# Mamba-2 scan and expert merge on one core: outputs of two pairs of chunks in one TensorE visit, the state term in 32x32 tiles

## The chip, the cores and the metric

One core of a Trainium2 chip. The metric is the device time of the kernel in microseconds (us), the median of several executions. TensorE is called PE here, VectorE DVE, ScalarE ACT, GpSimd POOL, and SyncE, which issues nearly all transfers, SP.

## The reference

Two parts run one after the other, all in float32. First a state-space scan (4 sequences, 8 heads, 768 positions, 32 channels and 16 states per head), written in chunks:

```python
L = np.exp(cum[:, :, :, None] - cum[:, :, None, :]) * causal   # decay from j to i
CB = np.einsum('bhin,bhjn->bhij', Cc, Bc)
y_intra = np.einsum('bhij,bhjd->bhid', CB * L, xc)
y_inter = np.einsum('bhin,bhnd->bhid', Cc, state) * np.exp(cum)[:, :, :, None]
y[:, :, sl] = y_intra + y_inter
state = decay_full[:, :, None, None] * state + np.sum(Bx, axis=2)
```

Then four experts over the 3072 rows of 256 values that the scan gives:

```python
p = domain_probs / (domain_probs.sum(-1, keepdims=True) + 1e-09)
for e in range(4):
    h = np.maximum(x @ w1[e], 0.0)          # 256 -> 1024
    out += p[:, e:e + 1] * (h @ w2[e])      # 1024 -> 256
```

## The kernel before

The scan runs in 24 chunks of 128 positions, numbered so that chunks 4i to 4i+3 are the i-th chunk of the four sequences. A chunk holds all 8 heads. Its work:

- `fetch` loads the chunk's x, B and C (tile xb), its decays spread over all partitions (ab) and, from chunk 4 on, its decays by head (ah).
- `decays` makes the decay matrix LT with two scans on DVE (L455), the decayed B in MT on POOL (`fade`, L461), the masked C in ctm on ACT (`mask`, L436), and from chunk 4 on the running decay dec (DVE, L735) and the decayed C, cts (POOL, L738).
- `scores` multiplies B and C on PE in four tiles of 32x128 (`score`, L443). It fills four PSUM banks with two chunks; then DVE multiplies each quarter of each chunk by LT into MT (`masked`, L600), eight instructions of 128x256 for a pair.
- `outputs` multiplies on PE, for two chunks: the state term, two 64x64 tiles a chunk (L774), and the part inside the chunk with the chunk's own new state, eight matmuls of 128x32 a chunk (`inner`, L468). ACT copies the outputs to yT (L790) and the new state to A (`keep_state`, L475 to L478).
- `carry` turns A on DVE (L806), adds the decayed old state (L808) and spreads the result S over a block-diagonal M by a product with qmask (L811), which the 64x64 tiles need, as two heads share a tile.

In odd chunks (`turned_round`) the halves of B, C and the decays are loaded the other way round, so that the odd chunk's state term uses the two 64x64 tiles that the even chunk leaves free.

The experts work on blocks of 4, 4, 4, 6 and 6 chunks (B, B, B, H, H) by a scheme that saves block products at the price of sums: sums of weights (L919), of tokens (L938) and of results (L857, L1136). Every product is L830, two matmuls of 128x128 by 128x256. ACT copies partial sums out of PSUM (snapshots, L839 and L1085) and into it (seeds, L844). DVE applies the gates (L865). Weights that are sums are stored once (L924) and loaded again (L916).

A block's work comes in units (a pair or a triple of weight blocks). `PAIRS_AT` says in which unit of a block the next block's pairs of chunks are made; within a unit the scores are put at position SC = 1 of the list of products and the outputs at OUT = 14:

```python
for x, make in ((SC, scores), (OUT, outputs)):
    mark = len(line)
    make(cs)
    at[x] = line[mark:]
```

The order of PE's work (`line`) is written out by this code. The order on every other engine is made by a planner (`Plan`) while the program is built: it walks through time with an assumed cost for each piece of work, assumed distances between engines (HOP), an assumed landing of transfers (RATE, LANDING) and an allowance after a landing before another engine's instruction on it is placed (MARGIN). It also hands out buffers: NV tiles v for values, NW tiles w for weights, eight PSUM banks. On the chip each engine takes its instructions strictly in the planned order.

Of the kernel before, what the change touches and what calls it, by code (L numbers as in the profile page):

```python
# [12 lines left out]
P = 128  # L13
# [5 lines left out]
HOP = 0.2  # L19
LANDING = 2.2  # L20
KEEP = 5
NV, NW = 33, 32
SC, OUT = 1, 14
# [4 lines left out]
RATE, MARGIN = 310.0, 4.0  # L28
AFTER = 1
HELD = ("x", "w"), (5, 8), (0, 7)  # L30
LAST = (0, 1), (0, 2), (1, 1), (1, 2), (0, 0), (1, 0)
LATE = (13, 2), (6, 9), (11, 4), (10, 12), (3,), (1, 14), ("x", "w"), (5, 8), (0, 7)
PAIRS_AT = {(3, 2): {0: 0, 1: 1}, (4, 2): {0: 0, 2: 1}, (4, 3): {0: 0, 1: 1, 2: 2},
            (6, 3): {0: 0, 2: 1, 3: 2}}
# [7 lines left out]
class Value:  # L42
    def __init__(self, kind, seeded=False, fills=True):
        self.kind, self.seeded, self.fills = kind, seeded, fills
        self.home, self.writers, self.readers, self.left, self.end = None, [], [], 0, 0.0

# [14 lines left out]
class Plan:  # L61
# [12 lines left out]
    def add(self, on, fn, reads=(), writes=(), part=(), lag=0.0, due=None, reuse=None, two=False,  # L74
            port=True, after=None, kb=0):
        w = Work(on, fn, lag)
        w.two, w.port, w.after, w.kb = two, port, after, kb
# [14 lines left out]
        for v in dict.fromkeys([*reads, *writes, *part]):  # L92
            w.touched.append(v)
            v.left += 1
# [8 lines left out]
    def times(self, line, at):  # L103
# [5 lines left out]
        for w in reversed(self.all):  # L109
            us = min(w.on.values()) + w.lag  # L110
            last = [f.latest - HOP for f in w.feeds]
            if "PE" in w.on:
                last.append(w.nominal + us)
            elif not last:
                last.append(t if w.due is None else w.due().nominal)
            w.latest = min(last) - us
# [46 lines left out]
    def run(self, line, at, begin):  # L163
# [17 lines left out]
        self.stall, self.port, self.bus = [], 0.0, 0.0  # L181
        while todo:
            e = min(t, key=lambda e: t[e])
            now = t[e]
            best, soon = None, None
            late = self.late = max(0.0, t["PE"] - line[head].nominal) if head < len(line) else 0.0
            for w in waiting[e]:
                if w.start is not None or e == "PE" and w.place != head:
                    continue
                ready = max([w.ready, w.after.nominal + late if w.after else 0.0] + [  # L190
                    n.end + (MARGIN if n.kb and e != "SP" else 0.0 if n.by == e and not n.kb else HOP)
# [19 lines left out]
                elif soon is None or when < soon:  # L211
                    soon = when
# [20 lines left out]
            if w.kb:  # L233
                self.bus = max(self.bus, t[e] + 1.6) + w.kb / RATE
                w.end = self.bus + .6
# [73 lines left out]
def kernel(  # L309
# [36 lines left out]
    def turned_round(c):  # L346
        return c >= NSEQ and c % 2 == 1
# [17 lines left out]
    def some(n, shape, name, pool=const):  # L365
# [9 lines left out]
        "LT": some(2, [P, NH, P], "LT"),  # L375
        "MT": some(2, [P, NH, P + N], "MT"),
        "ctm": some(2, [HN, NT, P], "ctm"),
        "cts": some(2, [HN, NT, P], "cts"),
        "dec": some(4, [HN, P], "dec"),
        "A": some(4, [P, NT, N], "A"),  # L380
        "S": some(6, [HN, D], "S"),
        "M": some(6, [HN, NQ, D], "M"),
# [8 lines left out]
    def load_tokens(c, xb):  # L391
        src = xbc[real(c)]
        if turned_round(c):
            nc.sync.dma_start(out=xb[:, :OBT], in_=src[:, :OBT])
            nc.sync.dma_start(out=xb[:HALF, OBT:], in_=src[HALF:, OBT:])
            nc.sync.dma_start(out=xb[HALF:, OBT:], in_=src[:HALF, OBT:])
        else:
            nc.sync.dma_start(out=xb, in_=src)
# [5 lines left out]
    def load_heads(c, ah):  # L404
        src = ac_d[real(c)].unsqueeze(1).to_broadcast([NH, N, P])
        if turned_round(c):
            nc.sync.dma_start(out=ah[:HALF], in_=src[NH // 2:])
            nc.sync.dma_start(out=ah[HALF:], in_=src[:NH // 2])
        else:
            nc.sync.dma_start(out=ah, in_=src)  # L410
# [38 lines left out]
    def quarter(c, r):  # L449
        q = r ^ 2 * turned_round(c)  # L450
        return slice(NT * q, NT * q + NT)

# [7 lines left out]
    def fade(c, MT, xb, LT):  # L460
        nc.gpsimd.tensor_mul(  # L461
            MT[:, :, P:], xb[:, OB:OB + HN].rearrange("p (h n) -> p h n", h=NH),
            LT[:, :, P - 1:P].to_broadcast([P, NH, N]))

    def inner(c, t, y, xb, MT, w, start):
        for q in range(NQ):
# [3 lines left out]
                rhs=MT[:, NT * q + t, 0:w], start=start, stop=True,  # L470
                tile_position=(0, 32 * q), skip_group_check=True)

    def keep_state(c, A, y):
        if c % 2:
            nc.scalar.copy(out=A[:HALF], in_=y[HALF:])  # L475
            nc.scalar.copy(out=A[HALF:], in_=y[:HALF])
        else:
            nc.scalar.copy(out=A, in_=y)  # L478
# [45 lines left out]
    qmask = const.tile([P, NQ, D], FP32)  # L524
    nc.vector.memset(qmask, 0.0)
    for q in range(NQ):
        nc.vector.memset(qmask[32 * q:32 * q + 32, q], 1.0)
# [61 lines left out]
    LT, MT, ctm = homes["LT"], homes["MT"], homes["ctm"]  # L589
# [74 lines left out]
    B512, B256 = {"DVE": .73, "POOL": 1.5}, {"DVE": .42, "POOL": .78}  # L664
# [7 lines left out]
    def dma(fn, n=1, kb=256, **kw):  # L672
        return plan.add({"SP": .38 * n}, fn, lag=LANDING + kb / 190, kb=kb, **kw)
# [15 lines left out]
    yT, gates, S, M = {}, {}, {}, {}  # L689
# [5 lines left out]
    st[3]["ab"] = plan.taken("ab", 0, now + 2)  # L695
    for c in range(2):
# [3 lines left out]
    def fetch(c):  # L700
        s = st[c]
        if "xb" not in s:
            s["xb"] = value("xb")
            dma(lambda e: load_tokens(c, s["xb"].t), 3 if turned_round(c) else 1, 320,
                part=[s["xb"]])
        if c >= NSEQ:
            s["ah"] = value("ah")
            dma(lambda e: load_heads(c, s["ah"].t), 2 if turned_round(c) else 1, 64,
# [5 lines left out]
    def decays(c):  # L714
        s = st[c]
        s["LT"] = value("LT")
        s["MT"] = value("MT")
        for part in range(2):
            if c < SPREAD:
                dve(1.25, lambda e, part=part: scan_quarters(  # L720
                    c, s["LT"].t, [b.t for b in s["a"]], part), reads=s["a"][2 * part:2 * part + 2],
                    part=[s["LT"]])
            else:
                half = NH * P // 2
                dve(1.25, lambda e, lo=half * part: scan(
                    s["LT"].t, s["ab"].t[:, lo:lo + half], lo), two=True, reads=[s["ab"]], part=[s["LT"]])
        if c < NCH - NSEQ:
            plan.add({"POOL": .43}, lambda e: fade(c, s["MT"].t, s["xb"].t, s["LT"].t),
# [671 lines left out]
```

## Time and profile before

| | |
|---|---|
| median of 3 runs | 631.25 us (630.66 to 634.42) |
| the profiled execution | 630.59 us, its span 628.8 us |
| PE busy | 622.6 us (99%) |
| DVE busy | 526.0 us (84%) |
| ACT busy | 261.9 us (42%) |
| POOL busy | 254.3 us (40%) |
| moved by DMA | 125.87 MB, mean 200 GB/s |

The span runs from the first to the last instruction. A group of the profile is named by its line in the kernel, its engine and operation, what it writes and reads, and its shape; the numbers are the busy time, the mean duration in ns, and the idle time of the engine just before it. In the chain of waits the last instruction is followed back to what released it. In the timeline each row has a start, a length, and a count of merged instructions; two records of PE belong to one float32 matmul.

### The profile page before, as it was taken

The page shows a single profiled execution, that of the slowest core. Times are in us where ns is not written, and L with a number is a line of the kernel's source. Part 1 is how long each engine was busy: PE and PEld are TensorE (multiplying, and loading weights), DVE is VectorE, ACT ScalarE, POOL GpSimd, SP SyncE. Part 2 cuts the span into 40 slices and gives each one's busy share as a digit, 9 for nine tenths or more (in the row PEclk, how much of TensorE's full clock was granted, in tenths as well). Part 3 has the DMA queues.
Part 4 walks back from the last instruction along what each step waited for, and adds up shares of the span by engine and source line. Part 5 has one row for each costly group of instructions (what it writes and reads, how often), then busy time and mean ns, then how long its engine had stood idle before and what let it go on. Part 6 is the DMA issues. An engine that isn't in the chain of part 4 may idle for free.

```text
span 628.8 us, 10190 instructions
## 1 busy us (share of the span) xinstructions
PE 622.6 (99%) x3363; PEld 529.3 (84%) x3363; DVE 526.0 (84%) x869; ACT 261.9 (42%) x538; POOL 254.3 (40%) x267
## 2 busy tenths in 40 slices
PE   9999999999999999999999999999999999999997
PEld 5787888888888888878888888888888888888886
DVE  7988899899997699988778988978787977768684
ACT  4222642434434353344433336355444235455441
POOL 4153552625534764543666421414045521233130
PEclk9999999999999999999999999999999999999999
DMA  7999795484898965699997827546123333951001
GB/s 206 307 304 346 231 302 197 123 282 126 287 336 298 315 189 164 173 322 334 349 365 244 280 63 250 176 118 199 57 80 94 101 73 80 361 176 47 1 1 51
DMA packets 110932, 125.87 MB, mean 200 GB/s; under 512 B 28692, under 2 KB 76832, under 8 KB 110880
## 3 DMA queue, kind: packets, MB, share of 16 engines
q1 hardware_dynamic: 110500, 124.97, 62.3%
q8 instruction: 27, 0.44, 0.3%
q10 hardware_dynamic: 380, 0.25, 0.1%
q14 instruction: 25, 0.20, 0.1%
HBM read 100.30 MB, written 24.89 MB: 199 GB/s over the span
## 4 chain that ended last, share of the span: by engine, by line
PE 93%; DMA 3%; DVE 2%; ACT 1%; issue 0%; SPq 0%; POOL 0%; ACTq 0%; POOLq 0%; DVEq 0%
PE bank L830 87%; PE bank L468 2%; DMA ab<-acut_d 2%; PE bank L443 2%; DMA w<-in_w_dram 1%; PE bank L774 1%; PE bank L603 1%; PE bank L580 0%; DVE LT L455 0%; DVE v L857 0%; DVE v L865 0%; POOL v L857 0%; DVE MT L600 0%; SPq L418 0%; DVE w L919 0%
## 5 line engine op out<-in xcount | busy, mean ns | idle before, releaser
L830 PE MATMUL bank<-v,w 128*128 128x256 f32 x1864 | 438.9, 380 | 0.0
L830 PEld LDWEIGHTS bank<-v,w 128*128 128x128 f32 x1864 | 352.1, 190 | 53.6 <-issue 4.0
L830 PE MATMUL bank<-Y,w 128*128 128x256 f32 x792 | 203.1, 379 | 1.2 <-ACT v L839 1.2
L857 POOL TENSOR_TENSOR v<-v,v 128x512 f32<-128x512 f32 x71 | 101.0, 1424 | 190.4 <-DVE v L857 84.4
L857 DVE TENSOR_TENSOR v<-v,v 128x512 f32<-128x512 f32 x199 | 162.8, 841 | 17.9 <-ACT v L839 14.5
L830 PEld LDWEIGHTS bank<-Y,w 128*128 128x128 f32 x792 | 150.1, 190 | 22.7 <-ACT v L839 2.0
L865 DVE SCALAR_TENSOR_TENSOR v<-bank,gate 128x512 f32<-128x512 f32 x172 | 116.7, 686 | 41.5 <-PE bank L830 34.2
L1085 ACT COPY v<-bank 128x512 f32<-128x512 f32 x107 | 62.6, 585 | 163.3 <-PE bank L830 161.9
L844 ACT COPY bank<-v 128x512 f32<-128x512 f32 (+1 forms) x192 | 108.1, 578 | 27.3 <-DVE v L857 24.4
L919 POOL TENSOR_TENSOR w<-w,w 128x256 f32<-128x256 f32 x102 | 89.9, 901 | 40.3 <-PE bank L830 29.6
L839 ACT COPY v<-bank 128x512 f32<-128x512 f32 x106 | 61.9, 585 | 100.7 <-PE bank L830 97.7
L455 DVE TENSOR_TENSOR_SCAN LT<-ab,ident 128x512 f32<-128x512 f32 x42 | 54.1, 1306 | 2.6 <-DMA ab<-acut_d 2.6
L857 DVE TENSOR_TENSOR v<-bank,v 128x512 f32<-128x512 f32 x40 | 27.6, 689 | 17.6 <-PE bank L830 16.4
L738 POOL TENSOR_TENSOR cts<-ctm,dec 128x256 f32<-128x256 f32 x20 | 19.1, 965 | 43.5 <-DVE dec L735 20.8
L1136 POOL TENSOR_TENSOR v<-v,v 128x256 f32<-128x256 f32 x20 | 17.1, 865 | 45.2 <-ACT v L1085 45.1
L600 DVE TENSOR_TENSOR MT<-bank,LT 128x256 f32<-128x256 f32 x93 | 32.1, 414 | 0.3
L436 ACT ACTIVATE ctm<-xb,tmask 128x128 f32<-128x128 f32 x48 | 15.9, 392 | 27.8 <-DMA w<-in_w_dram 9.8
L1136 DVE TENSOR_TENSOR v<-v,v 128x256 f32<-128x256 f32 x40 | 18.6, 493 | 4.6 <-ACT v L1085 4.3
L461 POOL TENSOR_TENSOR MT<-xb,LT 128x128 f32<-128x128 f32 x20 | 11.1, 566 | 21.9 <-DVE LT L455 20.7
L919 DVE TENSOR_TENSOR w<-w,w 128x256 f32<-128x256 f32 x36 | 17.4, 506 | 0.2
L990 DVE TENSOR_TENSOR bank<-bank,v 128x512 f32<-128x512 f32 x22 | 15.2, 691 | 2.6 <-PE bank L830 2.6
L919 POOL TENSOR_TENSOR w<-w 128x256 f32<-128x256 f32 x13 | 10.2, 790 | 17.4 <-DMA w<-in_w_dram 15.8
(76 smaller groups left out, 216.3 us busy)
## 6 DMA issues: line engine op xcount, KB each, us to landing
w<-in_w_dram SPq DMA_DIRECT2D x130, 256.0 KB
w<-w_d SPq DMA_DIRECT2D x130, 256.0 KB
w_d<-w SPq DMA_DIRECT2D x82, 256.0 KB
ab<-acut_d SPq DMA_DIRECT2D x21, 512.0 KB
w<-in_w_dram SPq DMA_DIRECT2D x38, 128.0 KB
xb<-in_xbc_dram SPq DMA_DIRECT2D x12, 320.0 KB
gate<-p_d SPq DMA_DIRECT2D x10, 384.0 KB
gate<-p_d SPq DMA_DIRECT2D x11, 256.0 KB
```

What stands on the lines that cost most here:

```text
L436: nc.scalar.mul(ctm[:, t], xb[:, OCT:OCT + P], tmask[:, t:t + 1])
L455: nc.vector.tensor_tensor_scan(out=LT.rearrange("p h s -> p (h s)")[:, lo:lo + w], data0=src, data1=ident.rearrange("p h s -> p (h s)")[:, ...
L600: nc.vector.tensor_mul(MT[:, h, 0:P], g, LT[:, h])
L738: plan.add({"POOL": .78}, lambda e: nc.gpsimd.tensor_mul(s["cts"].t, s["ctm"].t, s["dec"].t.unsqueeze(1).to_broadcast([HN, NT, P])), reads ...
L830: nc.tensor.matmul(out=o, lhsT=w[:, j], rhs=x if half is None else x[:, j], start=(start and j == 0), stop=(j == 1), skip_group_check=True)
L839: act(.6, lambda e: nc.scalar.copy(out=flat(v), in_=bank.t), reads=[bank], writes=[v])
L844: act(.6 if to > FB else .38, lambda e: nc.scalar.copy(out=bank.t[:, :to], in_=flat(v)[:, :to]), reads=[v], writes=[bank])
L857: plan.add(engines, lambda e: (on(e).tensor_add if sign > 0 else on(e).tensor_sub)(flat(v), whole(x), whole(y)), reads=[x, y], writes=[v], ...
L865: dve(.7 if x.kind == "bank" else .74, lambda e: nc.vector.scalar_tensor_tensor(out=h.t, in0=whole(x).rearrange("p (j m) -> p j m", j=JJ), ...
L919: plan.add({"POOL": .78} if due else B256, lambda e, r=r, x=x, y=y, sign=sign: (on(e).tensor_add if sign > 0 else on(e).tensor_sub)(view(r ...
L1085: act(.6, lambda e: nc.scalar.copy(out=flat(v), in_=bank.t), reads=[bank], writes=[v])
L1136: plan.add(engines, lambda e: (on(e).tensor_add if sign > 0 else on(e).tensor_sub)(o[1](), x[1](), y[1]()), reads=[v for v in vs if v is n ...
```

## The change

The state term is done in 32x32 tiles, one matmul for each of the four quarters of a chunk (two heads' states side by side in a quarter's 32 rows), straight from S; M and qmask go. The quarters of chunk c are turned by `turn_of(c)` = 0, 2, 1, 3 quarters, so that four chunks take the 16 tiles of the array, each its own. Loads of B, C and decays are split at the turn, and `keep_state` turns the new state back in as many copies as it needs. The decay matrices of a pair of chunks lie side by side in one tile (LT, MT), odd chunks with their heads moved by half, so that one DVE instruction of 128x512 masks a bank for both chunks. `PAIRS_AT` now lists single steps: in the first three transitions between blocks two pairs share one step for outputs, and so do the second and third pair of a three-pair block after a four-unit block. The planner gets new assumed costs, distances and transfer limits, and there are fewer tiles v and w.

```diff
-HOP = 0.2
+HOP = 0.06
+D512, D256 = .64, .36
-NV, NW = 33, 32
-SC, OUT = 1, 14
+NV, NW = 31, 28
-RATE, MARGIN = 310.0, 4.0
+RATE, MARGIN = 330.0, 2.0
+HOLD = 12.0
+NEAR, WORTH = .0, 1.0
+WAIT = .15
+LANES, ISSUE = 8, .48
-PAIRS_AT = {(3, 2): {0: 0, 1: 1}, (4, 2): {0: 0, 2: 1}, (4, 3): {0: 0, 1: 1, 2: 2},
-            (6, 3): {0: 0, 2: 1, 3: 2}}
+PAIRS_AT = {
+    (3, 2): ((0, 1, "s0"), (1, 1, "s1"), (1, 14, "o01")),
+    (4, 2): ((0, 1, "s0"), (2, 1, "s1"), (2, 14, "o01")),
+    (4, 3): ((0, 1, "s0"), (0, 14, "o0"), (1, 1, "s1"), (2, 1, "s2"), (2, 14, "o12")),
+    (6, 3): ((0, 1, "s0"), (0, 14, "o0"), (2, 1, "s1"), (2, 14, "o1"), (3, 1, "s2"), (3, 14, "o2")),
+}
...
-    def turned_round(c):
-        return c >= NSEQ and c % 2 == 1
+    def turn_of(c):
+        return (0, 2, 1, 3)[c % NSEQ]
+    def turned(c):
+        lo = P // NQ * turn_of(c) if c >= NSEQ else 0
+        return [(lo, 0, P - lo), (0, P - lo, lo)][:1 + (lo > 0)]
...
-        "LT": some(2, [P, NH, P], "LT"),
-        "MT": some(2, [P, NH, P + N], "MT"),
-        "ctm": some(2, [HN, NT, P], "ctm"),
-        "cts": some(2, [HN, NT, P], "cts"),
-        "dec": some(4, [HN, P], "dec"),
+        "LT": some(1, [P, 2, NH, P], "LT"),
+        "MT": some(2, [P, 2, NH, P + N], "MT"),
+        "ctm": some(4, [HN, NT, P], "ctm"),
+        "cts": some(4, [HN, NT, P], "cts"),
+        "dec": some(8, [HN, P], "dec"),
         "A": some(4, [P, NT, N], "A"),
-        "S": some(6, [HN, D], "S"),
-        "M": some(6, [HN, NQ, D], "M"),
+        "S": some(10, [HN, D], "S"),
...
     def keep_state(c, A, y):
-        if c % 2:
-            nc.scalar.copy(out=A[:HALF], in_=y[HALF:])
-            nc.scalar.copy(out=A[HALF:], in_=y[:HALF])
-        else:
-            nc.scalar.copy(out=A, in_=y)
+        x = turn_of(c)
+        n = (P, P // NQ, HALF, P // NQ)[x]
+        for here in range(0, P, n):
+            there = (here + P // NQ * x) % P
+            nc.scalar.copy(out=A[here:here + n], in_=y[there:there + n])
...
         for r in (3, 2, 0, 1):
-            for j, c in enumerate(cs):
-                s = st[c]
-                dve(.42, lambda e, c=c, r=r, s=s, j=j: masked(
-                    c, r, s["MT"].t, s["LT"].t, gs_[r].t, j), reads=[gs_[r], s["LT"]],
-                    part=[s["MT"]])
+            def fn(e, r=r):
+                g = gs_[r].t.rearrange("p (c t s) -> p c t s", c=2, t=NT)[:, :len(cs)]
+                js, h = slice(cs[0] % 2, cs[0] % 2 + len(cs)), quarter(cs[0], r)
+                nc.vector.tensor_mul(s["MT"].t[:, js, h, 0:P], g, s["LT"].t[:, js, h])
+            dve(D512 if len(cs) > 1 else D256, fn, reads=[gs_[r], s["LT"]], part=[s["MT"]], hold=HOLD)
...
-                for h in range(2) if c >= NSEQ else ():
-                    rows = slice(HALF * h, HALF * h + HALF)
-                    to = HALF * (1 - h if turned_round(c) else h)
+                for r in range(NQ) if c >= NSEQ else ():
+                    rows, to = slice(32 * r, 32 * r + 32), 32 * ((r + turn_of(c)) % NQ)
                     nc.tensor.matmul(
-                        out=v[to:to + HALF, :, 0:P],
-                        lhsT=M[c - NSEQ].t.rearrange("p q d -> p (q d)")[rows, rows],
+                        out=v[to:to + 32, :, 0:P], lhsT=S[c - NSEQ].t[rows],
                         rhs=st[c]["cts"].t[rows], start=True, stop=False,
-                        tile_position=(HALF * h, to), skip_group_check=True)
+                        tile_position=(32 * r, to), skip_group_check=True)
...
-            nc.vector.tensor_mul(M[c].t, t.unsqueeze(1).to_broadcast([HN, NQ, D]), qmask)
-        dve(.82 if more else .54, fn, two=True, reads=[s["A"], *more], writes=[S[c], M[c]])
+        dve(.45 if more else .25, fn, two=True, reads=[s["A"], *more], writes=[S[c]])
...
-            p = PAIRS_AT[len(of_block), blocks[k + 1].scheme.pairs].get(i)
-            if p is not None:
-                cs = [blocks[k + 1].first + 2 * p + j for j in range(2)]
-                for c in cs:
-                    fetch(c)
-                    decays(c)
-                for x, make in ((SC, scores), (OUT, outputs)):
-                    mark = len(line)
-                    make(cs)
-                    at[x] = line[mark:]
-                    del line[mark:]
-                for c in cs:
-                    carry(c)
+            for unit, x, what in PAIRS_AT[len(of_block), blocks[k + 1].scheme.pairs]:
+                if unit != i:
+                    continue
+                cs = [blocks[k + 1].first + 2 * int(p) + j for p in what[1:] for j in range(2)]
+                mark = len(line)
+                if what[0] == "s":
+                    for c in cs:
+                        fetch(c)
+                        decays(c)
+                    scores(cs)
+                else:
+                    outputs(cs)
+                    for c in cs:
+                        carry(c)
+                at[x] = line[mark:]
+                del line[mark:]
```

In the planner, transfers are now issued in pieces over LANES queues of which each holds one until it has landed, work on PE has an end 0.16 us after its slot and work on the other engines 0.09, a mask is wanted within HOLD of its scores, and most assumed costs are a little lower (512-wide DVE work .64 for .70 to .73, ACT copies .5 for .6, POOL sums of 256 .72 for .78).

## The prediction

> **What bounds the kernel now.** I read the page first (busy times, then the chain that ended last), then the chain in order of time, then PE's own waits, then short stretches of the timeline.
>
> ```profile
> span 628.8 us, 10190 instructions
> PE 622.6 (99%) x3363; PEld 529.3 (84%) x3363; DVE 526.0 (84%) x869; ACT 261.9 (42%) x538; POOL 254.3 (40%) x267
> PE 93%; DMA 3%; DVE 2%; ACT 1%; issue 0%; SPq 0%; POOL 0%; ACTq 0%; POOLq 0%; DVEq 0%
> ```
>
> TensorE works 99% of the span. The chain leaves it only near the start, around 268 us and at the end. PE's waits say how little that costs:
>
> ```profile
> PE bank L830 <- ACT v L839: 1.2, 2, 0.7
> ```
>
> So no engine but PE has anything to give: taking away DVE, POOL or DMA work can win back about 1.2 us of PE waits and no more. What can shorten the kernel is PE's own work. The chain shows it piece by piece (start, length, what):
>
> ```profile
> 42.61 8.90 PE bank L830 x40
> 51.51 0.59 PE bank L774 x8
> 52.10 1.12 PE bank L468 x32
> 53.22 8.03 PE bank L830 x36
> 61.26 1.08 PE bank L443 x16
> 62.33 11.42 PE bank L830 x52
> 73.75 0.59 PE bank L774 x8
> 74.35 1.12 PE bank L468 x32
> 75.46 37.32 PE bank L830 x172
> ```
>
> L830 is the expert matmuls. They are cut ten times by a visit for scores (L443) and ten times by a visit for outputs (L774, the state term, then L468, the part inside the chunk), two chunks each. A record of L830 costs (37.32-11.42)/(172-52) = 0.2158 us; a run of 52 then has 11.42-52x0.2158 = 0.20 us left over. That is the price of coming back to L830 once. A visit for outputs of two chunks therefore costs 0.59+1.12+0.20 = 1.91 us, ten of them 19.1 us. Inside a visit:
>
> ```profile
> 51.13 0.38 PE L830 MATMUL bank<-Y,w 128*128 128x256 f32 x1
> 51.44 0.45 PE L774 MATMUL bank<-cts,M 64*64 64x256 f32 x4
> 51.71 0.40 PE L774 MATMUL bank<-cts,M 64*64 64x256 f32 x4
> 52.03 0.33 PE L468 MATMUL bank<-MT,xb 128*32 128x144 f32 x4
> 52.18 0.43 PE L468 MATMUL bank<-MT,xb 128*32 128x144 f32 x8
> 52.30 0.43 PE L468 MATMUL bank<-MT,xb 128*32 128x144 f32 x8
> 52.43 0.43 PE L468 MATMUL bank<-MT,xb 128*32 128x144 f32 x8
> ```
>
> Each fp32 matmul leaves two records (two passes). The four 64x64 tiles of the two chunks (the odd chunk's halves are turned round, so they take the other two tiles) start within 0.02 us and run at once: the state term of both chunks lasts as long as that of one. In L468 four tiles start together, and the next four 0.1225 us later (52.18, 52.30, 52.43).
>
> **The Trainium skill.** "TensorEngine Tiling (Array Packing)", Key Properties, says that changing the tiling mode drains the engine, and that 32x32 mode has 16 tiles. The trace agrees on the drain: the steps into L774, into L468 and back are 0.31, 0.32 and, with the slow first record, 0.30 us where a record takes 0.216. "TensorE: Matmul & The Clock Gate", Part 3 (Measured speedup vs the span model), gives tiles that run at once about 4 ns each; here they start about 7 ns apart, for four tiles. For 16 it gives a measured 10.6x; no run here shows 16. "SBUF — State Buffer" says that VectorE with two SBUF inputs and GpSimd hold a shared port pair by turns. That fits L857: 841 ns mean on DVE with two SBUF inputs, 689 ns when one input is a bank.
>
> **The change, part by part.** My sum is against the profiled execution: span 628.8, own time 630.59 us. The median of the runs is 631.25, 0.66 us more.
>
> (1) *One visit for two pairs.* The two programs' PE order shows visits for outputs falling from ten to seven: the first three blocks hand on with one visit of four chunks each, one such visit comes out of the step from the third to the fourth block, and four visits of two chunks stay. (By steps: 2 to 1, 2 to 1, 3 to 2, 3 to 3.) So three visits go. Scores keep ten. For a visit of four chunks: entry as before. State term: 16 tiles of 32x32, each chunk on its own diagonal, so no two matmuls share a tile. The first pass's starts take 16x0.007 = 0.11 us; the second pass can begin when tile 0 is done, 0.216 us plus its weights' load (0.05 us for 64 columns here, 0.03 for 32 by the same rate), as the 0.27 us from 51.44 to 51.71 is made up; then 15x0.007 = 0.10 until the last start and 0.31 to L468. Sum 0.216+0.03+0.10+0.31 = 0.65 us, against 0.59 for two chunks. L468 adds eight groups of four: 8x0.1225 = 0.98. The visit: 1.91+0.06+0.98 = 2.95, against 2x1.91 = 3.82. Saved 0.87 each, 2.6 us in three.
> Bounds, as the trace shows only four tiles at once: the state term free of any addition, 2.8 us; if the four matmuls that read one strip of rows go two by two, two passes of 0.216 more per visit, 1.3 us; all four by turns, 1.3 us per visit, a loss of 1.3 us. The four tiles of L468 read the same rows with four different moving operands at once, so I take 2.6.
>
> (2) *Two-chunk visits in 32x32 tiles.* Eight tiles for four: four starts more (0.03 us), a shorter load (-0.02): 0.0 for the four visits.
>
> (3) *Masks by pairs, M gone.* On DVE the 80 masks of 128x256 that are paired become 40 of 128x512. Row: 32.1 us for 93, 0.345 each, so 27.6 us go; 40x0.68 (L865, also one bank input: 116.7/172) = 27.2 come. Nothing won there. M<-S,qmask (L811, x20) takes 6.8 us with it. But the order shows 20 more sums of 128x512 on DVE and 20 fewer on POOL: +16.8 by 841 ns, -28.5 by 1424. DVE goes from 526 to about 534-537, POOL down to about 225. None of it is on the chain; DVE's cover is PE's 99%. It is gone if DVE fills a stretch: in the table of windows DVE is already busy 27.3 of the 29.4 us from 13.2 to 42.6.
>
> (4) *State turned by quarters.* keep_state goes from 28 to 53 copies on ACT: +25x0.18 = 4.5 us of 262, beside 58% idle time. In a visit of four chunks ACT gets 4 output copies (0.37) and 11 small ones (0.18), 3.5 us in a row. Snapshots and seeds queue behind them. In the new order seven of the eleven small copies stand behind the next snapshots and seed, so I take 0; at worst 0.5 us per visit, 1.5.
>
> (5) *Issues on SP:* 651 to 666, 15 more by quarters. SP waits for buffers, it isn't full: 0.
>
> (6) *Fewer buffers, new distances (HOP, D512, MARGIN, RATE).* W goes from 32 to 28 and V from 33 to 31. I counted, in both orders, the L830 work between a stored sum's load and its first matmul: median 39 us before and 37 after, the shortest 19 and 12. Loads near the crowded start took 5.5 to 6.4 us on the chain, so that still covers them. DVE sums stand at least 2.2 us ahead of their matmul (1.7 before). The first outputs move from 42 to 62 us of PE work, so the first pair's masks aren't urgent any more. Both PE stalls of before have ACT's masks (L436) queued ahead of a snapshot (L839) that PE needs:
>
> ```profile
> 41.40 0.69 ACT L436 ACTIVATE ctm<-xb,tmask 128x128 f32<-128x128 f32 x2 [1.72 <-DMA xb<-in_xbc_dram]
> 42.61 0.70 PE L830 MATMUL bank<-Y,w 128*128 128x256 f32 x2 [0.53 <-ACT v L839]
> ```
>
> Two such stalls cost 1.2 us. The new order might lose them or make others: bounds -1.2 and +2; I take -0.3.
>
> Sum: 630.59-2.6-0.3 = 627.7 for the profiled execution; with the 0.66, a median of 628.3 us, -0.5%.
>
> **Rivals.**
> *A, the 16 tiles don't all run at once.* For: 16 isn't shown. Against: L468. At the two-by-two bound 629.6, at the worst 632: within 1%. Chance 0.15.
> *B, the slower side: consumers stand too close to their loads.* MARGIN falls from 4 to 2 us, so scans (L455) and masks (L436) may be queued up to 2 us earlier; each blocks its engine's queue while its load is late, and a seed or snapshot behind it stops PE. For: it is what the two stalls are made of, and DMA is at 0.9 of its time in early slices. Place: the ten fetches of a pair. If each stalls PE for 1.2 us, 628.3+12 = 640; it ends slower by over 1% once a fetch costs 0.9 us. Against: the second stall waited 4.6 us for POOL, not for a load, and those two are all the trace has. Chance 0.10.
> *C, all stalls go too.* 631.25-2.8-1.2 = 627.2, still within 1%. Chance 0.12. For faster by over 1% (624.9) there is nothing left on PE to take: 0.03.
> The forecast itself: 0.60.
>
> **How the numbers follow.** About 1% (6.3 us) is what a measurement of this kernel can tell from no change. Forecast, A and C are within it: 0.87. B gives slower 0.10. The range: 626.0 below (C, less a spread between runs of 0.2%), 633.5 above (A's worst and the 1.5 for ACT).
>
> **What would show it.** Right: seven visits in the chain, three of them with about 0.65 us for 32 state records and 2.1 for 64 of L468; ten visits of 1.08 for scores; PE waits under 2 us; DVE busy 525-540 and POOL near 225. Wrong in step 1: a state term over 1 us. Wrong in step 6: PE waits of several us, released by ACT v or DVE v behind a late xb or ab. The prediction is wrong if PE's idle time grows by over 6 us, or if PE's own work falls by more than 4.

## The result and the profile after

The changed kernel takes 636.55 us (median of 6 runs, 634.32 to 637.49) against 631.26 us before (median of 6 runs, 630.66 to 634.42): ratio 1.0069, 95% interval 1.0042 to 1.0095. It is slower, by 5.3 us or 0.8% on the medians, and lies above the predicted range. The ratio is not that of the medians; the means, 636.15 and 631.80 us, give it. The profiled execution took 636.64 us, 6.05 us more than that of before; its span of 634.9 us is 6.1 us longer.

First the page of the changed kernel, span, busy times and the chain that ended last by engine:

```profile
span 634.9 us, 10315 instructions
PE 623.9 (98%) x3443; PEld 531.0 (84%) x3443; DVE 518.2 (82%) x823; ACT 267.2 (42%) x563; POOL 231.0 (36%) x256
PE 92%; DVE 3%; DMA 3%; issue 1%; SPq 0%; ACT 0%; DVEq 0%; ACTq 0%
```

No other engine has become full: DVE, expected at 534 to 537, is at 518 us. But PE's idle time has grown from 628.8-622.6 = 6.2 us to 634.9-623.9 = 11.0 us, and PE is busy 1.3 us longer although three visits, 2.6 us, are gone. Both want an explanation. The line numbers have moved: products L830 are L872 now, scores L443 are L477, the state term L774 is L818, the inner part L468 is L510.

The chain in order of time, at a visit of four chunks and at one of two (start, length, what):

```profile
80.06 0.64 PE bank L818 x32
80.71 2.11 PE bank L510 x64
...
236.19 0.59 PE bank L818 x16
236.78 1.12 PE bank L510 x32
```

So the visits are as foreseen: 16 tiles take 0.64 us, eight tiles 0.59. PE's two costliest waits (what waits, for what: total, times, longest):

```profile
PE bank L872 <- DVE v L907: 3.3, 1, 3.3
PE bank L510 <- DVE MT L796: 1.9, 2, 1.7
```

Before, the longest was 0.7 us. The timeline around the long wait, with the idle time before an instruction and its releaser in brackets:

```profile
54.61 2.76 SPq L444 DMA_DIRECT2D ah<-ac_d  x4
...
60.84 0.42 DVE L778 TENSOR_TENSOR_SCAN dec<-ah,zeros 128x128 f32<-128x128 f32 x1 [2.24 <-DMA ah<-ac_d]
61.18 0.67 DVE L907 SCALAR_TENSOR_TENSOR v<-bank,gate 128x512 f32<-128x512 f32 x1
61.90 1.65 PE L872 MATMUL bank<-v,w 128*128 128x256 f32 x3 [3.33 <-DVE v L907]
```

The wait is put down to the gate (L907), which reads a bank that the next product writes. But the gate itself waited for nothing except its turn: ahead of it in DVE's queue stood a scan of decays (L778) that only a later output visit needs, and that scan waited 2.24 us for its load. The chain puts that load's way from issue to landing at 5.53 us ("55.22 5.53 DMA ah<-ac_d" is the piece). This is the pattern to look for: the line that releases PE is innocent, and the one before it on the same engine shows the DMA.

The same stretch in the table of windows (PE, PEld, DVE, ACT, POOL busy, then PE's mean clock, DMA share and GB/s), as a whole and in three parts:

```profile
55.00:70.00 15.00, 11.67 (x52) 8.60 (x51) 10.95 (x21) 0.84 (x2) 5.81 (x8) 0.77 0.89 290
55.00:60.80 5.80, 3.58 (x17) 2.81 (x15) 3.21 (x6) 0.59 (x1) 1.24 (x3) 1.00 0.96 293
60.90:67.60 6.70, 5.70 (x16) 3.91 (x20) 5.95 (x13) 0.00 (x0) 2.23 (x3) 0.50 0.91 308
67.70:70.00 2.30, 2.30 (x23) 1.77 (x20) 1.63 (x3) 0.26 (x1) 2.25 (x3) 1.00 0.69 228
```

The clock is full up to 60.8 us, half until 67.6 and then full again. PE starts again at 61.9, so it works at half clock for 5.7 us: the records of L872 start 0.427 us apart instead of 0.216 until 67.4. Against the same work in the profile of before this costs 2.8 us, and it counts as *busy* PE. That is the main reason why PE's busy time did not fall with the visits: the idle stretch is paid a second time, as slow work.

The account of the 6.1 us, from gaps between PE records beyond their usual spacing: the first product 0.4 us later; gaps of 1.8 us at 22.8 (masks L796 behind the row scan of their chunk), 3.5 at 58.2, 0.7 at 114.6 and 0.4 at 150.3; half clock 2.8; less 2.6 for the visits, less 1.5 for the two gaps of before. That is 5.5; the other 0.6 us are in small delays that I did not follow one by one. The gap at 22.8 hangs on a row of decays that was stored 0.9 us later than in the profile of before. The next two experiments keep the plan up to there, and their profiles don't have this gap, so it is owed to the execution and not to the plan.

### The profile page after: what moved, and what is told of

Same layout as the page of the kernel before. It is cut to its first block, busy times and chain, and to the rows that moved or that the text cites. A ratio compares the mean times of both kernels' runs of the same rounds, so it can differ in the third digit from the quotient of the medians.

```text
span 634.9 us, 10315 instructions
## 1 busy us (share of the span) xinstructions
PE 623.9 (98%) x3443; PEld 531.0 (84%) x3443; DVE 518.2 (82%) x823; ACT 267.2 (42%) x563; POOL 231.0 (36%) x256
## 3 DMA queue, kind: packets, MB, share of 16 engines
q1 hardware_dynamic: 111300, 124.97, 61.6%
## 4 chain that ended last, share of the span: by engine, by line
PE 92%; DVE 3%; DMA 3%; issue 1%; SPq 0%; ACT 0%; DVEq 0%; ACTq 0%
PE bank L872 86%; PE bank L477 2%; PE bank L510 2%; DMA acut_d<-a_cut 1%; DMA ab<-acut_d 1%; DMA ah<-ac_d 1%; DVE LT L494 1%; PE bank L642 1%; DVE v L899 1%; PE bank L818 1%; DVE v L907 1%; DVE w L961 0%; DMA w_d<-w 0%; DVE dec L778 0%; PE bank L1250 0%
## 5 line engine op out<-in xcount | busy, mean ns | idle before, releaser
L872 PE MATMUL bank<-v,w 128*128 128x256 f32 x1864 | 441.6, 382 | 3.6 <-DVE v L907 3.3
L872 PEld LDWEIGHTS bank<-v,w 128*128 128x128 f32 x1864 | 353.7, 191 | 58.1 <-issue 4.9
L872 PE MATMUL bank<-Y,w 128*128 128x256 f32 x792 | 203.2, 379 | 0.5 <-ACT bank L886 0.5
L899 DVE TENSOR_TENSOR v<-v,v 128x512 f32<-128x512 f32 x219 | 174.9, 826 | 22.9 <-ACT v L881 20.2
L872 PEld LDWEIGHTS bank<-Y,w 128*128 128x128 f32 x792 | 150.2, 190 | 21.9 <-ACT bank L886 0.9
L907 DVE SCALAR_TENSOR_TENSOR v<-bank,gate 128x512 f32<-128x512 f32 x172 | 116.7, 682 | 43.7 <-PE bank L872 38.6
L899 POOL TENSOR_TENSOR v<-v,v 128x512 f32<-128x512 f32 x51 | 73.3, 1440 | 192.7 <-DVE v L907 121.7
L961 POOL TENSOR_TENSOR w<-w,w 128x256 f32<-128x256 f32 x106 | 92.6, 894 | 76.7 <-PE bank L872 48.9
L899 DVE TENSOR_TENSOR v<-bank,v 128x512 f32<-128x512 f32 x40 | 27.4, 684 | 7.4 <-PE bank L872 6.8
L796 DVE TENSOR_TENSOR MT<-bank,LT 128x512 f32<-128x512 f32 (+1 forms) x48 | 28.4, 633 | 0.7 <-PE bank L477 0.7
L961 POOL TENSOR_TENSOR w<-w 128x256 f32<-128x256 f32 x14 | 12.5, 896 | 41.6 <-DMA w<-in_w_dram 32.4
L504 POOL TENSOR_TENSOR MT<-xb,LT 128x64 f32<-128x64 f32 (+1 forms) x28 | 14.2, 516 | 33.6 <-DVE LT L494 33.4
L1178 POOL TENSOR_TENSOR v<-v,v 128x256 f32<-128x256 f32 x16 | 15.2, 968 | 27.4 <-DVE v L1178 19.8
L781 POOL TENSOR_TENSOR cts<-ctm,dec 128x256 f32<-128x256 f32 x20 | 17.4, 886 | 4.3 <-DVE dec L778 3.3
```

Source lines behind the costliest of these rows:

```text
L781: plan.add({"POOL": .72}, lambda e: nc.gpsimd.tensor_mul(s["cts"].t, s["ctm"].t, s["dec"].t.unsqueeze(1).to_broadcast([HN, NT, P])), reads ...
L796: nc.vector.tensor_mul(s["MT"].t[:, js, h, 0:P], g, s["LT"].t[:, js, h])
L872: nc.tensor.matmul(out=o, lhsT=w[:, j], rhs=x if half is None else x[:, j], start=(start and j == 0), stop=(j == 1), skip_group_check=True)
L899: plan.add(engines, lambda e: (on(e).tensor_add if sign > 0 else on(e).tensor_sub)(flat(v), whole(x), whole(y)), reads=[x, y], writes=[v], ...
L907: dve(D512, lambda e: nc.vector.scalar_tensor_tensor(out=h.t, in0=whole(x).rearrange("p (j m) -> p j m", j=JJ), scalar=0.0, in1=g.t[:, 2 * ...
L961: plan.add({"POOL": .72} if due else B256, lambda e, r=r, x=x, y=y, sign=sign: (on(e).tensor_add if sign > 0 else on(e).tensor_sub)(view(r ...
```

## The experiments

The kernel before was timed again beside each of four groups of experiments; its medians there were 630.90, 630.82, 631.82 and 631.06 us. A difference of medians between two groups is thus uncertain by about 1 us. The ratio is to the kernel before of the same group.

**Is it this one scan?** The two scans of chunks 9 and 10 are put about 9 us later in the finished order, into two more tiles for their loads.

```diff
+    spare = some(2, [HN, P], "ah_more")
+    for c, tile_ in zip((9, 10), spare):
+        w = st[c]["scan"]
+        st[c]["ah"].home = Home(tile_)
+        done.remove(w)
+        first = min(done.index(f) for f in w.feeds)
+        done.insert(min(first, next(i for i, x in enumerate(done) if x.start > w.start + 9.0)), w)
```

> The changed kernel's order of everything, but the two running-decay scans of chunks 9 and 10 (DVE, L778), whose small loads land late, stand about nine further pieces of DVE work back, with two more ah tiles so that the loads keep their place. Theory 1 (a scan queued too close behind its load holds the DVE queue, the gate behind it holds a PSUM bank, and PE stands 3.3 us and then runs about 4.5 us at half clock): the 3.3 us wait and the half clock go, about 5.6 us, so 631 us (630 to 632.5). Rival 1 (DVE is simply late in that stretch, whatever stands first): the wait returns at the next gate, 635 to 637. Rival 2 (the loss sits in the start, in the landing of the decays' store): 635 or more, with the first outputs of chunk 3 as late as before.

Measured: 636.19 us, ratio to before 1.0083 (1.0065 to 1.0100). Nothing is won. The timeline of this kernel shows who took the place:

```profile
62.16 0.43 DVE L961 TENSOR_TENSOR w<-w,w 128x256 f32<-128x256 f32 x1 [2.90 <-DMA w<-in_w_dram]
62.51 0.68 DVE L907 SCALAR_TENSOR_TENSOR v<-bank,gate 128x512 f32<-128x512 f32 x1
```

Now a sum of weights stands ahead of a gate and waits 2.90 us for another load. More than one load of this stretch is late for its consumer, and moving one scan only moved the wait to the next.

**What does the clock cost?** The changed kernel with four matmuls on nothing, 128x512 into bank 0, ahead of the product that waits. They fill the idle time and no more.

```diff
+        if w is held:
+            for _ in range(4):
+                idle(BANK[0])
```

> The changed kernel with four idle matmuls of 128x512 (3.4 us of PE) put in front of the product that waits for the bank, so that PE is busy while it waits. Theory 1's second half (the wait costs its length and then about 2.3 us of half clock): the clock stays at full, 636.5 - 2.3 = 634.2. If the slow matmuls after the wait have another reason than the idle time: 636.5 and the same slow stretch.

Measured: 633.99 us (632.76 to 636.35), ratio 1.0064 (1.0045 to 1.0082), 2.6 us below the changed kernel's median. The window that had 0.77:

```profile
55.00:70.00 15.00, 14.42 (x69) 10.43 (x69) 12.37 (x22) 3.52 (x6) 7.20 (x9) 1.00 0.82 274
```

The product still starts only at 60.0 us, 3.7 us after the product before it as in the changed kernel, but the clock stays at 1.00. The clock of the runs that were not profiled says the same: its mean over a run is 0.994 to 0.997 in all six runs of the changed kernel and 0.998 to 1.000 in all six of this one. So of what the one late scan costs, 2.6 us by the medians, and 2.8 by the records above, is half clock and not waiting. (The ratios, 1.0069 and 1.0064, differ by less: each has other runs of before beside it, one of 634.42 us among the six beside the changed kernel.) The Trainium skill, "TensorE: Matmul & The Clock Gate", Part 1 (What's actually happening), tells of half rate after an idle window of about 3.4 us. Here a shorter wait is enough, as the run with MARGIN 2 and old costs below shows.

**Is it the margin?** MARGIN is the time that the planner keeps between the planned end of a load and the start of its consumer, and also before a buffer that a transfer used last is written again. Four runs change it alone, two on each kernel:

```diff
-RATE, MARGIN = 330.0, 2.0
+RATE, MARGIN = 330.0, 4.0      (6.0 in the other)
```

> The changed kernel planned with MARGIN 4.0 as in the kernel before, nothing else. The shortest distance from an ah load to its scan in the crowded stretch grows from 3.5 us of PE work to 6. Theory 1: a landing of 4.4 to 5.5 us fits in 6, so that wait is gone: 630 to 632, with PE waits under 2 us in all. Rival 3 (the new order as such, its costs and HOP, makes the stalls): 634 to 638.

> The changed kernel planned with MARGIN 6.0, nothing else. With 2.0 it took 636.55 us and with 4.0 632.16. Theory 1 (consumers queued too close behind loads that land 4.5 to 7 us after their issue in the first 63 us): the stalls of the 4.0 plan, some 5 us, shrink to about 2.5, so 629.5 (628 to 631), below the kernel before. Rival 3 (the stalls come from the new costs and HOP): 632 to 634, as with 4.0.

and on the kernel before:

```diff
-RATE, MARGIN = 310.0, 4.0
+RATE, MARGIN = 310.0, 2.0      (6.0 in the other)
```

> The kernel before, planned with MARGIN 2.0 instead of 4.0. Theory 1 in its narrow form (two quarters of C and B and more small loads in the new structure bring the loads late, and MARGIN 2 then lets the scans follow too closely): in this order the ah loads stand 7 us or more ahead of their scans, so 631 to 632.5. If MARGIN alone is the cause: 634 or more.

> The kernel before, planned with MARGIN 6.0; with 2.0 it took 632.59 and with 4.0 630.9 us. It has some 1.2 to 1.5 us of PE waits left, so theory 1 gives 629.5 to 631. If a longer allowance costs by itself (work put later than it could be): 632 or more.

Measured medians, with the ratio to the kernel before as it is:

| MARGIN | kernel before | changed kernel |
|---|---|---|
| 2 | 632.59, 1.0032 (1.0021 to 1.0042) | 636.55, 1.0069 (1.0042 to 1.0095) |
| 4 | 631.26 | 632.16, 1.0017 (1.0001 to 1.0033) |
| 6 | 629.22, 0.9970 (0.9961 to 0.9980) | 631.15, 1.0007 (0.9997 to 1.0018) |

More margin helps both: from 2 to 6 by 5.4 us in the changed kernel and 3.4 in the one before on the medians, by 0.0062 (3.9 us) in both on the ratios. So it is not shown that the changed kernel gains more from it. The theory's numbers were met only roughly: 632.16 and 631.15 lie just above its ranges (630 to 632 and 628 to 631), 629.22 just below (629.5 to 631), and 632.59 just above its 632.5 for MARGIN 2, below the rival's 634. DVE's waits for transfers fall with it, which speaks for the loads: 12.9 us in all in the changed kernel, 8.1 with MARGIN 4 and 4.3 with MARGIN 6.

With 6, the kernel before has no gap over 0.35 us left after the first microsecond. In the changed kernel gaps of 0.4 to 0.9 us remain, about 3.7 us in all, and only one has a load in it. Its timeline at one of them:

```profile
298.76 1.92 DVE L494 TENSOR_TENSOR_SCAN LT<-ab,ident 128x512 f32<-128x512 f32 x1
300.59 3.95 DVE L899 TENSOR_TENSOR v<-v,v 128x512 f32<-128x512 f32 x3
302.33 0.73 PEld L872 LDWEIGHTS bank<-v,w 128*128 128x128 f32 x4 [1.09 <-DVE v L899]
```

A row scan, 1.21 us elsewhere, lasts 1.92 us while POOL adds (L899, two of them in 3.42 us from 298.32), and the combining sums queued behind it come late, 1.3 us each. The plan reckons 1.15 us for such a scan and 0.64 for a sum, so a margin for loads doesn't mend that: DVE gets too little time. So the margin is the larger part of the loss, but not all: the 2.6 us of the visits are still missing.

**Were the merged visits won at all?** The changed kernel with MARGIN 4 and ten output visits again:

```diff
-    (3, 2): ((0, 1, "s0"), (1, 1, "s1"), (1, 14, "o01")),
+    (3, 2): ((0, 1, "s0"), (0, 14, "o0"), (1, 1, "s1"), (1, 14, "o1")),
...
```

> The changed kernel planned with MARGIN 4.0, but with every pair's outputs in a visit of its own (ten visits instead of seven), all in 32x32 tiles. By step 1 of the prediction PE's own work grows by three visits of 0.87, 2.6 us, from the 632.16 of the merged plan to 634.8 if the stalls stay the same; each visit of two chunks lasts 0.59 and 1.12 us in the chain. If merging is what crowds the loads, stalls fall by as much and it stays at 631 to 632.

Measured: 632.34 us, 1.0019 (1.0007 to 1.0030), against 632.16 merged. Nothing is left of 2.6 us, as the rival theory had it: behind the start the merged kernel's profile has 5.4 us of gaps, this one's 2.6. On these planner costs the saving is given back as waits.

**Are the short costs the rest?** The changed kernel with MARGIN 4 and the planner's main numbers of before. "Old costs" below means these alone; the planned costs of ACT, POOL and the row scans, the transfers in pieces and HOLD stay as changed:

```diff
-HOP = 0.06
-D512, D256 = .64, .36
-RATE, MARGIN = 330.0, 2.0
-WAIT = .15
+HOP = 0.2
+D512, D256 = .72, .42
+RATE, MARGIN = 310.0, 4.0
+WAIT = .2
...
-        w = Work(on, fn, (.16 if "PE" in on else .09) if lag is None else lag)
+        w = Work(on, fn, 0.0 if lag is None else lag)
...
-                    n.end + (MARGIN if n.kb and e != "SP" else -n.lag if n.by == e == "PE" else HOP)
+                    n.end + (MARGIN if n.kb and e != "SP" else 0.0 if n.by == e and not n.kb else HOP)
```

> The changed kernel planned with the main figures of the kernel before: MARGIN 4.0, HOP 0.2, RATE 310, 0.72 and 0.42 us for DVE work of 512 and 256, no lag after PE and the other engines. Theory 1: the costs hardly matter, 631 to 633, as the changed costs with MARGIN 4.0 (632.16). Rival 3 (tighter costs and distances make the stalls): 629 to 630.

Measured: 632.48 us, 1.0016 (0.9998 to 1.0033), no better, but with runs from 629.22 to 634.20. The profiled one, 632.14 us, has a single large wait, and it is at the start:

```profile
17.99 1.23 DVE L494 TENSOR_TENSOR_SCAN LT<-ab,ident 128x512 f32<-128x512 f32 x1 [2.06 <-DMA ab<-acut_d]
19.13 1.39 DVE L796 TENSOR_TENSOR MT<-bank,LT 128x256 f32<-128x256 f32 x4
20.34 0.93 PE L510 MATMUL bank<-MT,xb 128*32 128x144 f32 x16 [2.87 <-DVE MT L796]
```

Chunk 3's row scan waits for its row of decays and stands ahead of chunk 2's masks, for which PE waits 2.87 us; 3.4 us at half clock follow (21.6 to 25.0), which cost 1.7. The cause is one number: the row's arrival is given to the planner as 2 us after the plan's start at 13.2 us, and under these costs the scan fits ahead of the masks. After it, one gap of 0.8 us is all. So the next two runs took MARGIN 6, and the second also told the planner of a later row:

```diff
-RATE, MARGIN = 310.0, 4.0
+RATE, MARGIN = 310.0, 6.0
...
-    st[3]["ab"] = plan.taken("ab", 0, now + 2)
+    st[3]["ab"] = plan.taken("ab", 0, now + 6)      (second run only)
```

> The changed kernel with the costs, transfer rate and distances of the kernel before, and MARGIN 6 in place of 4. Theory (the loss of the changed kernel lies in what its planner leaves between a load and its consumer, and in which work it puts ahead of a needed gate; the short costs of the new version make its plan too tight): chunk 3's lower-triangle scan is again ahead of chunk 2's masks at the start, which cost 2.95 us and 1.4 us of half clock in the profiled run of the same costs with MARGIN 4, and beyond that stalls under 1 us in all: 630 us. Rival (what is left over the 629.2 us of the kernel before with MARGIN 6 is owed to the fewer tiles, or to the form of the masks and of the state copy, and the costs are innocent): 631.2 us, as the changed kernel with MARGIN 6, with 3 us or more of stalls after 30 us.

> As the run with the old costs and MARGIN 6, and the planner is told that chunk 3's row of decays lands at 6 us, not at 2 us, so that its scan is planned behind the first gate and chunk 2's masks. Theory: the stall at 17 us and the half clock behind it go, 3 to 4 us in such runs as have them; the three visits saved (2.6 us) then show against the 629.2 us of the kernel before with MARGIN 6: 627 us, 626.5 to 628.2. Rival (the saved visits are given back whatever the plan, since the stalls come from somewhere else): 629.5 us or more, with new stalls of over 2 us.

Measured: 629.51 us, 0.9971 (0.9958 to 0.9984), with the start wait in its profile (2.5 us, then 3.4 us at half clock). Nine of its 22 runs have a mean clock of 0.995 to 0.997, as the profiled one, and take 630.2 to 632.8 us; the other 13, at 0.999 or more, take 627.6 to 629.9. With the later row 627.25 us (626.83 to 628.18), 0.9929 (0.9910 to 0.9947). None of its six runs is under 0.998. This beats both kernels and the 629.22 us of before with MARGIN 6. Its page and all but the shortest of PE's waits:

```profile
span 625.1 us, 10332 instructions
PE 620.0 (99%) x3443; PEld 529.4 (85%) x3443; DVE 516.7 (83%) x808; ACT 266.1 (43%) x563; POOL 245.7 (39%) x271
PE bank L642 <- PEq L1437: 0.8, 1, 0.8
PE bank L477 <- ACT p_sb L605: 0.3, 1, 0.3
```

PE is busy 620.0 us, 2.6 less than before, as much as the three visits. The waits that are left are of the start and were there before.

**Does the saving show once the waits are gone?** The same kernel with ten output visits, the edit of above:

> As the run before it (old costs, MARGIN 6, the row of decays at 6 us), but with the output visits of the kernel before, one for each pair of chunks: three state visits of 16 tiles and their inner loads more. Theory: 2.6 us more than the merged kernel of the same call, 629 to 630 us: with a plan that leaves no stalls the merging brings what the work removed says. Rival (the merged visits ask for the masks of two pairs at once and pay with stalls what they save): equal to the merged kernel within 1 us.

Measured: 629.46 us, 0.9959 (0.9944 to 0.9973), PE busy 622.6. Merging brings 629.46-627.25 = 2.2 us here, and brought nothing with the tight plan. The rival is out for this plan. Without the merging it is level with the kernel before with MARGIN 6 (629.22 us): what the change wins is the merging.

**Do the fewer tiles cost?** The kernel before, MARGIN 6, with the changed kernel's tiles:

```diff
-NV, NW = 33, 32
+NV, NW = 31, 28
```

> The kernel before with MARGIN 6 and with the tiles of the changed kernel (NV 31 for 33, NW 28 for 32), nothing else. Theory (margin and costs decide, six tiles fewer cost nothing with MARGIN 6): 629.2 us as with all its tiles, 628.7 to 629.8. Rival (fewer homes for the inputs press the loads towards their consumers and are what keeps the changed kernel with MARGIN 6 at 631.15 us): 631 to 632 us, with waits of VectorE or GpSimd for w loads that the run with all tiles does not have.

Measured: 630.89 us (630.21 to 631.27), 0.9977 (0.9967 to 0.9988). That is 1.7 us over the one with all tiles by the medians and near the rival, but only 0.0007 (0.4 us) by the ratios, as the kernel before was 1.0 us slower in this group; what the tiles cost is between the two. It is not by the waits that the rival asked for: GpSimd waits 10.1 us in all for loads and stores of w, against 18.2 with all tiles, and VectorE for none. Its profile has one gap of 1.5 us, at 401, that the other has not. The chain to it:

```profile
400.61 0.70 DVE v L865
401.41 1.30 DVE v L857 x2
```

Here the sum that PE waits for stands behind a second gate (L865) and another sum; with all tiles it stands ahead of that gate. Fewer tiles gave another order, and that order costs the gap. Since the 627.25 us kernel has the same few tiles, they are no bound by themselves.

**Which of the numbers?** Four more runs around the 627.25 us kernel: MARGIN 2; rate 330; the changed engine costs kept, with rate 310, MARGIN 6 and the later row; MARGIN 8.

> As the 627.25 us kernel (old costs and rate, row of decays at 6 us), but with MARGIN 2, the margin of the change. Theory 1 (the margin alone makes the loss: consumers stand at the head of their queues while loads are under way): 631 to 634 us, with waits of ACT and DVE for DMA back and stalls of 4 us or more in the first 70 us. Theory 2 (the short engine costs and the rate made it, and a plan on the old costs forgives a margin of 2): 627.5 to 629 us.

> As the 627.25 us kernel, but with the transfer rate of the change (330), so that of the change's planner numbers only the rate stays. If the engines' costs (distance, DVE times, waits) are what keeps the changed kernel with MARGIN 6 at 631.15 us: 627 to 628.3 us. If the rate is: 630 to 631.5 us.

> The changed kernel with MARGIN 6 and the rate of before (310), its engine costs as changed (row of decays at 6 us). If the engines' short costs leave needed gates and combines behind scans and sums: 630.3 to 631.5 us with stalls of DVE and ACT origin, none for loads. If the rate is the cause: 627 to 628.3 us.

> As the 627.25 us kernel, but MARGIN 8. Its profile shows no stalls left behind the start, so that more room has nothing to give: 627.2 us, 626.8 to 628. If late loads still cost something in the runs that were not profiled: 626.5 us and a narrower spread. If loads that must be earlier collide with the stores: 628.5 us or more.

Measured:

| run | us | ratio to before |
|---|---|---|
| old costs, MARGIN 2 | 630.42 (627.36 to 634.03) | 0.9994 (0.9975 to 1.0013) |
| old costs, rate 330 | 627.35 | 0.9945 (0.9925 to 0.9965) |
| changed costs, rate 310 | 629.61 | 0.9981 (0.9969 to 0.9992) |
| old costs, MARGIN 8 | 629.34 | 0.9971 (0.9961 to 0.9981) |

The rate is innocent beside the old costs. The engine costs are not: at MARGIN 6, with rate 310 and the later row in both, they make 629.61-627.25 = 2.4 us, and 629.61-627.35 = 2.3 against the run of the same group, where the expectation had 3 or more; 629.61 lies between its two ranges. MARGIN 2 alone, on good costs, brings 3.2 us back, less than the first theory said and more than the second. Its runs are 6.7 us apart: eight with a mean clock of 0.999 or more take 627.4 to 630.5 us, six with 0.995 to 0.997 take 631.7 to 634.0. The profiled one, at 0.997, shows again the late load, then the clock:

```profile
52.47 5.12 DMA ah<-ac_d
...
59.49 2.67 PE bank L872 x6
```

The window behind the wait:

```profile
59.80:63.20 3.40, 3.40 (x9) 2.70 (x8) 2.64 (x7) 0.00 (x0) 0.79 (x1) 0.50 1.06 390
```

A PE wait of 2.1 us, shorter than the 3.4 us named above, is followed by 3.4 us at half clock. MARGIN 8 was expected to change nothing and is 2.1 us slower: its profile has three gaps of 0.5 to 0.8 us, put down to sums and seeds. A planner's order changes as a whole with any number, and the time with it by up to about 2 us here, so differences of that size between two plans are not a price of the number that was turned. The 2.4 us of the engine costs are hardly more than that, so their part is likely but not proven; the 2.2 us of the merging stand besides in PE's busy time.

## Why the prediction was wrong

- **Step 1, right.** 0.64 us for 16 tiles (0.65 predicted), 2.11 for the inner part (2.1), ten visits of scores left. The 2.6 us saved stand in PE's busy time of the 627.25 us kernel, 2.2 of them in the time. The mechanism holds too: the first 16 records of the state term start within 0.10 us (79.995 to 80.095), about 7 ns apart, and the second pass starts 0.24 us after the first. Rival A is out.
- **Step 2, right.** 0.59 us before and after.
- **Step 3, right in kind.** The 20 sums did move from POOL to DVE (219 for 199). They came cheaper, 12.1 us for the group where 16.8 was reckoned, at 826 ns each for 841. DVE as a whole came out at 518 us, some 16 below the forecast; the rest of that was not followed up.
- **Steps 4 and 5** cost nothing that a trace shows: in the changed kernel's profile no PE wait is put down to a copy of `keep_state`, and the 627.25 us kernel has all of these copies and issues.
- **Step 6 failed.** It stood at -0.3 us with an upper bound of +2. It was about +8: the measured +5.3 us on the medians plus the 2.6 that the visits save. Three things went wrong in it. First, I measured the room between loads and *matmuls* (weights), where nothing became short, and held the 5.5 to 6.4 us that loads of w and ab took on the old chain against that room alone, not against the room of the loads that DVE and ACT consume (ah, ab, xb). In the profile of before the shortest time from the issue of an ah load to its scan is 6.4 us (23.7 to 30.1), and the scan finds it landed. In the changed kernel one scan was ready for its load 3.4 us after the issue (55.2 to 58.6), and the load took 5.5. Second, a wait was priced as the wait alone; its half clock, 2.8 us, was not in the sum at all. Third, the shorter engine costs were passed over as assumptions; at MARGIN 6 the runs with them take about 2.4 us more.
- **Its own signs** were mixed. A PE wait of several us, released by DVE v behind a late load, came as described for a failed step 6, only that the load was one of ah and not of xb or ab. PE's idle time grew by 4.8 us, under the 6 that was to show the forecast wrong: that sign left out that the second half of the price counts as busy time.
- **Rival B had the mechanism**, named the queue behind a late load, the scans and the margin, and had 0.10. Its price was wrong in form: not ten fetches of 1.2 us each, but one wait of 3.3 us with half clock behind it and a few short ones. At its true size, +5.3 us, it lies under the 1% from which it was counted as slower, and above the range, which ended at 633.5 because step 6 was bounded at +2. The argument against it, that only two stalls were in the old trace, was weak: these two were made under MARGIN 4.

Taken apart, the 9.3 us between the changed kernel and the 627.25 us one are 5.4 us for the margin (2 to 6, on changed costs) and 3.9 for costs and the later row; in the other order of edits the margin is 3.2. All of these are differences of medians between groups, good to about 1 us. What each engine cost (distance, DVE time, lag) does alone was not tried. Nor was it shown how much of the margin's effect comes from loads and how much from the buffers that transfers used last, which the same number guards.

## What to carry to other kernels

When a change tightens a plan's distances, compare for each load that an in-order engine consumes the room before its consumer with the time such loads really take to land in that stretch, and look at what is queued behind the consumer: that is what pays. To an idle stretch of TensorE of 2 us or more add the half clock behind it: here it cost another 1.7 to 2.8 us, set by the work that fell into it and not by the length of the wait alone. And where a saving of certain size doesn't arrive, loosen the plan before giving up the saving: here it was there, hidden under waits that the same edit had made.

## What the runs showed of the hardware

After TensorE waits of 2.1, 2.5, 2.9 and 3.3 us the granted clock was half (0.50 in the windows); after waits of 1.7 us (changed kernel, at 22.8) and 1.6 us (two other runs) it stayed at 1.00. The stretch at half clock did not grow with the wait in step: it was 3.4 us long in the three runs with 2.1, 2.5 and 2.9 us (59.8 to 63.2, 20.6 to 24.0, 21.6 to 25.0), and 6.8 us in the changed kernel (60.9 to 67.7) and in the one with two scans later (61.6 to 68.4, a wait of 2.9 with one of 1.0 before it). It costs about half of the part in which TensorE has work: an estimated 1.7 us in the first three (half of 3.4), and 2.8 in the changed kernel against the same work before. Idle matmuls in the wait kept the clock at 1.00.

Sixteen fp32 tiles of 32x32 run together in 0.64 us, 0.05 more than eight. Small loads (pieces of ah of 16 to 64 KB, 5.1 and 5.5 us from issue to landing) are about as slow as ab's of 512 KB (5.1 to 7.0 us on the chains) when the DMA engines are 0.92 to 0.96 busy.

A row scan on DVE from SBUF takes 1.18 to 1.23 us in all 441 cases of the 18 profiles in which no GpSimd instruction ran beside it. Of the 315 with one beside them 105 took over 1.5 us, and up to 2.3. This agrees with what the prediction cites on the port that the two engines share (section "Who interferes with whom" of that page); what sets these cases apart from the other 210 is not shown.
